# Moving the helper sums of an attention and PReLU kernel to VectorE, giving attention fixed units, and regrouping on ScalarE

## The chip, the cores and the metric

The kernel runs on one core of a Trainium2 chip. A core has five engines that run their own instruction streams in order and wait for each other through semaphores: TensorE (PE in the profile, its weight loads PEld), VectorE (DVE), ScalarE (ACT), GpSimd (POOL) and SyncE (SP). The metric is device time of one execution in microseconds. Before the change the median of 10 runs is 315.63 us (314.99 to 317.3).

## The reference

Attention without a softmax, with a norm on each head's output, then a two-layer PReLU network over the concatenated heads. All inputs are float32, the output is float32 of 4608 x 512.

```python
batch, n_heads, seq, head_dim = (8, 8, 576, 64)
kv  = einsum('bhsd,bhse->bhde', k, v)
o   = einsum('bhsd,bhde->bhse', q, kv)
o   = o / sqrt(mean(o*o, -1) + 1e-6) * g_norm
x   = o.transpose(0, 2, 1, 3).reshape(4608, 512)
h   = x @ w_in                                # 512 -> 2048
g   = maximum(h, 0) + alpha * minimum(h, 0)
out = g @ w_out                               # 2048 -> 512
```

## The kernel before

The 4608 tokens are cut into 9 blocks of 512 (w = 0 to 8); the tokens of a block can come from two of the eight batches. Everything on TensorE is fp16, accumulated in fp32.

**Attention of a block** goes by four head pairs j, each in four steps. `step_t` (L232) transposes q of the pair with 5 matmuls into `qt_ps`, and ACT copies it to `qt_sb`. `step_kv` (L250) makes k^T v with 5 matmuls into `kv_ps`, and DVE masks it into `kv_sb`. `step_ot` (L268) makes the outputs with 2 matmuls into `ot_ps`, and ACT squares them (`sq_sb`). `step_ssq` (L286) sums the squares with one matmul into `ssq_ps`, ACT makes the reciprocal root (`rstd`), and DVE writes the normed block part `xt`. `window_steps` (L308) lists these 16 steps in one order, in which the last `ssq` follows the last `ot` directly. From stage two on `qt_ps` and `kv_ps` share the one PSUM bank of the pool `ps_s`; `ssq_ps` has the bank of `ps_q` up to the loop of block 1, and from the loop of block 2 that of `ps_s` as well.

**First layer of a block**: 16 units. `m1_group` (L351) runs 4 matmuls of 512 columns into a bank `h_ps`; ACT makes `m_sb = relu(-h)` (L342) and DVE writes the activation `gt = beta * m_sb + h` in fp16 (L346). A bank can be filled again when DVE has read it. There are three banks until block 2, and two (`h0`, `h1`) from then on.

**Second layer of block 0**: four output tiles of 128 tokens, 16 matmuls each. Three (`ya`, `yb`, `yc`, AHEAD = 3) run in "stage two", between the first layers of blocks 0 and 1, with the attention steps of block 1 in between; the fourth (`y_ps`) runs in the loop of block 1.

**Second layer of blocks 1 to 8**: by Winograd's form of Strassen's product, with 7 products of 16 matmuls of 256 columns (`prod_mm`, L461) into three banks yX, yY, yZ. The products need sums of parts of the weights (`w_sum`, L404: 4 kinds in two halves) and of parts of the activations (`s_sum`, L428: 4 kinds for 4 parts, so 16 for a block). In the loop of block w each unit has one `m1_group` of block w, the sums that are due, 7 matmuls of the products of block w - 1, a read of a finished bank (`y_read`, L494), and attention steps of block w + 1, popped from their list as the units go by. After block 8 a tail runs its products alone.

**Where the sums run before**: on POOL all eight `w_sum` (L407 to L419; the third kind overwrites part of `w_out_sb`), all sums of the third kind (L437), and in block 1 those of the fourth kind (L440). The others run on DVE (L433, L435, L440).

**Loading**: `load_batch(b)` issues six DMAs from the POOL queue (three of 64 KB for the last 64 rows, three of 512 KB). k and q arrive head by head, and `regroup` (L142) copies them into the order that the matmuls need: of batches 0 and 1 on DVE, of batch 2 on POOL after stage two (`regroup_batch`, L155), of later batches on POOL in units 10 and 12 of the loop of block b - 2, one copy of 2048 elements a partition for k and one for q. POOL thus has, in one in-order stream, DMA issues, regroup copies and sums. Results are stored from the SP queue.

Of the kernel before, what the change touches and what calls it, by code (L numbers as in the profile page):

```python
# [17 lines left out]
def kernel(  # L18
# [11 lines left out]
    nc = tc.nc  # L30
# [111 lines left out]
    def regroup(b, nm, h0, h1, eng=None):  # L142
        dst = bufs[b % NBUF][nm][:, 0:TPP, h0:h1, :].rearrange("p t h d -> p h t d")
        src = stages[b, nm][:, h0:h1, :, :]
        if eng is nc.scalar:
            nc.scalar.copy(out=dst, in_=src)
        else:
            (eng or nc.vector).tensor_copy(out=dst, in_=src)
# [247 lines left out]
    def w_lo(i, c0, c1):  # L396
        return w_out_sb[i][:, :, c0:c1]
# [3 lines left out]

    def w_sum(n, i):
        sl = slice(i * GW, (i + 1) * GW)
        if n != 3 and n not in wsum:  # L404
            wsum[n] = w_p.tile([P, NK, HC], FP16, name=f"wsum{n}")
        if n == 1:
            nc.gpsimd.tensor_sub(  # L407
                out=wsum[1][:, sl, :], in0=w_lo(i, HC, D_MODEL), in1=w_lo(i, 0, HC)
            )
        elif n == 2:  # L410
            nc.gpsimd.tensor_sub(  # L411
                out=wsum[2][:, sl, :], in0=w_hi(i, HC, D_MODEL), in1=wsum[1][:, sl, :]
            )
# [12 lines left out]
    def s_sum(w, n, k):  # L426
        lo, hi = gts[w, k], gts[w, k + KQ]
        a11, a21 = lo[:, :, 0:HW], lo[:, :, HW:W]  # L428
        a12, a22 = hi[:, :, 0:HW], hi[:, :, HW:W]
        t = sum_p.tile([P, 2, HW], FP16, name=f"s{n}", tag=f"s{n}{k}", bufs=1 if n == 2 else 2)  # L430
        sums[w, n, k] = t
        if n == 1:
            nc.vector.tensor_add(out=t[:], in0=a21, in1=a22)  # L433
        elif n == 2:
            nc.vector.tensor_sub(out=t[:], in0=sums[w, 1, k][:], in1=a11)  # L435
# [25 lines left out]
    def prod_mm(w, n, i):  # L461
        a, c = divmod(i, NK)
        bank, fresh = y_bank(w, {1: "X", 2: "X", 6: "Y", 7: "Y", 4: "Y", 5: "Z", 3: "Z"}[n], a)
        cols = slice(a * P, (a + 1) * P)
        hi_cols = slice(HW + a * P, HW + (a + 1) * P)
        k, r = divmod(c, 2)
        if n == 1:
            lhs = gts[w, k][:, r, cols]
        elif n == 2:
            lhs = gts[w, k + KQ][:, r, cols]  # L470
        elif n == 4:
            lhs = gts[w, k + KQ][:, r, hi_cols]
        else:
            lhs = sums[w, {6: 2, 7: 3, 5: 1, 3: 4}[n], k][:, r, cols]
        q, rr = divmod(c, GW)
        if n == 1:
            rhs = w_out_sb[q][:, rr, 0:HC]
        elif n == 2:
            rhs = w_out_sb[q + WQ // 2][:, rr, 0:HC]
        elif n == 3:  # L480
            rhs = w_out_sb[q + WQ // 2][:, rr, HC:D_MODEL]
        elif n == 7:
            rhs = w_out_sb[q][:, rr, HC:D_MODEL]
        else:
            rhs = wsum[{4: 4, 5: 1, 6: 2}[n]][:, c, :]
        nc.tensor.matmul(  # L486
            out=bank, lhsT=lhs, rhs=rhs, start=fresh, stop=(c == NK - 1), skip_group_check=True,
        )
# [80 lines left out]
    for g in range(3, NF):  # L569
# [5 lines left out]


    AHEAD = 3
    ys = [
        ps_y.tile([P, W], FP32, name="ya", tag="y"),
        h_bank("yb"),  # L580
        h_bank("yc"),
    ]
    steps = window_steps(1)
    n = len(steps)
    for g in range(NF):
        for a in range(AHEAD):
            y_mm(ys[a], 0, a, g)
            if a != 1 and steps and n - len(steps) < n * (AHEAD * g + a + 1) // (AHEAD * (NF - 3)):
                steps.pop(0)()
    for a in range(AHEAD):  # L590
        y_out(ys[a], 0, a)
    regroup_batch(2)

    def unit_sums(w, u):
        k, r = divmod(u, 4)
        k -= 1
        if k >= 0 and r < 3:
            s_sum(w, (1, 2, 4)[r], k)
            if r == 0:
                s_sum(w, 3, k)  # L600

    for w in range(1, NW):
        steps = window_steps(w + 1) if w + 1 < NW else []
        n = len(steps)
        first_g = 4 if w == 1 else 0
        if w == 2:
            h_tags[0] = ("h0", "h1")
            ssq_pool[0] = (ps_s, "s")
            for i in range(2):
                w_sum(3, i)  # L610
        if 0 < w and w + 2 < B:
            load_batch(w + 2)
        if w == 1:
            for i in range(2):
                for m in (1, 2, 4):
                    w_sum(m, i)
        y = None
        for u in range(NF):
            m1_group(w, G_ORDER[u])
            unit_sums(w, u)  # L620
            if w > 1 and u < 3:
                unit_sums(w - 1, NF + u)
# [63 lines left out]
```

## Time and profile before

| | us |
|---|---|
| median of 10 runs | 315.63 |
| the profiled execution | 316.04 |
| its span (first to last instruction) | 314.2 |
| PE busy | 283.9 (90%) |
| DVE busy | 218.4 (70%) |
| ACT busy | 161.0 (51%) |
| POOL busy | 128.1 (41%) |

Two clocks must be kept apart: the time that is measured (316.04 us for the profiled execution) and the span inside it (314.2 us) in which positions are given; the 1.84 us around it belong to both kernels. Positions below are microseconds from the span's start. A matmul's time in the profile runs until its modelled end, and matmuls overlap, so what a group of matmuls costs is read from the distance between starts. The same holds, to a smaller degree, for instructions that follow each other on DVE and ACT. The granted TensorE clock was 0.987 over the span.

### The profile page before, as it was taken

How to read it: one execution, taken by the hardware profiler on the slowest of the kernel's cores; microseconds unless marked ns; L12 is line 12 of the kernel's file. 1: busy time of each engine (PE TensorE's matmuls, PEld its weight loads, DVE VectorE, ACT ScalarE, POOL GpSimd, SP SyncE). 2: the span in 40 equal slices, each digit the busy share in tenths (PEclk: the TensorE clock that was granted, in tenths of full speed). 3: DMA queues.
4: the chain of work that ended last, by engine and by line, in shares of the span. 5: the costliest groups of instructions: out<-in, count | busy, mean ns of one | idle time of the engine just before them, and what ended most of it. 6: DMA issues, size and time to landing. Idle time of an engine off the chain costs nothing.

```text
span 314.2 us, 5166 instructions
## 1 busy us (share of the span) xinstructions
PE 283.9 (90%) x1972; PEld 180.1 (57%) x1972; DVE 218.4 (70%) x373; ACT 161.0 (51%) x268; POOL 128.1 (41%) x118
## 2 busy tenths in 40 slices
PE   5778999696697999999999999999999999999992
PEld 1523454343374657665766576656665666666682
DVE  4358833778768886888688768876777778866831
ACT  3246556385454556555655555555654565434210
POOL 8434412999999551365136413311111112211100
PEclk9599999999999999999999999999999999999999
DMA  7999999790039299029902990111102110200233
GB/s 110 180 206 195 200 198 215 106 158 2 33 28 183 52 144 182 2 40 156 167 18 26 157 162 9 26 67 34 37 1 52 50 33 11 75 19 33 63 89 85
DMA packets 52552, 28.32 MB, mean 90 GB/s; under 512 B 15136, under 2 KB 52016, under 8 KB 52528
## 3 DMA queue, kind: packets, MB, share of 16 engines
q0 software_dynamic: 40320, 18.16, 45.9%
q1 hardware_dynamic: 11424, 9.19, 10.3%
q10 hardware_dynamic: 784, 0.66, 0.8%
q8 instruction: 15, 0.25, 0.3%
q14 instruction: 9, 0.07, 0.1%
HBM read 36.71 MB, written 9.44 MB: 147 GB/s over the span
## 4 chain that ended last, share of the span: by engine, by line
PE 63%; DMA 14%; POOL 11%; DVE 4%; issue 4%; ACT 2%; DVEq 0%; POOLq 0%
PE h_ps L335 28%; PE yY L486 11%; PE yZ L486 9%; PE yX L486 8%; DMA qst<-in_q_dram 5%; DMA kst<-in_k_dram 5%; DMA vst<-in_v_dram 3%; PE qt_ps L236 2%; PE kv_ps L254 2%; PE ssq_ps L293 2%; PE ot_ps L277 2%; POOL wsum L407 1%; POOL wsum L411 1%; POOL wsum L415 1%; ACT m_sb L342 1%
## 5 line engine op out<-in xcount | busy, mean ns | idle before, releaser
L335 PE MATMUL h_ps<-xt,w_in_sb 128*128 128x512 f16 x576 | 146.1, 379 | 2.2 <-DVE gt L346 1.2
L346 DVE SCALAR_TENSOR_TENSOR gt<-m_sb,beta_sb,h_ps 128x512 f16<-128x512 f32 x144 | 107.1, 745 | 57.5 <-ACT m_sb L342 55.9
L342 ACT ACTIVATE m_sb<-h_ps 128x512 f32<-128x512 f32 x144 | 85.9, 597 | 78.5 <-PE h_ps L335 71.0
L437 POOL TENSOR_TENSOR s<-gt 128x512 f16<-128x512 f16 x32 | 39.0, 1219 | 134.0 <-DVE gt L346 133.7
L335 PEld LDWEIGHTS <-w_in_sb 128*128 128x128 f16 x576 | 54.2, 98 | 54.0 <-issue 9.8
L486 PEld LDWEIGHTS <-s 128*128 128x128 f16 x512 | 50.1, 98 | 22.9 <-DVE u L501 1.9
L486 PEld LDWEIGHTS <-gt 128*128 128x128 f16 x384 | 37.6, 98 | 14.8
L303 DVE SCALAR_TENSOR_TENSOR xt<-ot_ps,g2col,rstd 128x512 f16<-128x512 f32 x36 | 26.9, 747 | 12.5 <-ACT rstd L295 12.4
L486 PE MATMUL yX<-w_out_sb,gt 128*128 128x256 f16 x256 | 35.1, 273 | 0.0
L295 ACT ACTIVATE rstd<-ssq_ps,eps_t 128x512 f32<-128x512 f32 x36 | 24.7, 687 | 17.0 <-PE ssq_ps L293 16.8
L283 ACT ACTIVATE sq_sb<-ot_ps 128x512 f16<-128x512 f32 x36 | 21.3, 598 | 16.1 <-PE ot_ps L277 16.1
L248 ACT COPY qt_sb<-qt_ps 128x576 f16<-128x576 f16 x28 | 17.9, 638 | 18.4 <-PE qt_ps L236 18.4
L236 PE MATMUL qt_ps<-ident,qsb 128*128 128x128 f16 x160 | 14.9, 231 | 7.5 <-DVE kv_sb L262 4.2
L486 PE MATMUL yY<-w_out_sb,s 128*128 128x256 f16 x128 | 18.7, 272 | 1.7 <-DVE u L501 1.6
L440 DVE TENSOR_TENSOR s<-gt,s 128x512 f16<-128x512 f16 x28 | 19.4, 692 | 0.0
L433 DVE TENSOR_TENSOR s<-gt 128x512 f16<-128x512 f16 x32 | 19.3, 602 | 0.0
L293 PE MATMUL ssq_ps<-sq_sb,mask 128*128 128x512 f16 x36 | 13.9, 386 | 5.9 <-ACT sq_sb L283 4.5
L236 PEld LDWEIGHTS <-qsb 128*128 128x128 f16 x160 | 12.0, 103 | 11.4 <-issue 4.8
L486 PE MATMUL yZ<-w_out_sb,s 128*128 128x256 f16 x128 | 17.5, 272 | 0.7 <-DVE y_sb L513 0.3
L486 PE MATMUL yY<-wsum,s 128*128 128x256 f16 x128 | 17.6, 273 | 0.0
L486 PE MATMUL yY<-wsum,gt 128*128 128x256 f16 x128 | 17.6, 273 | 0.0
L486 PE MATMUL yZ<-wsum,s 128*128 128x256 f16 x128 | 17.6, 273 | 0.0
(66 smaller groups left out, 263.5 us busy)
## 6 DMA issues: line engine op xcount, KB each, us to landing
out_dram<-y_sb SPq DMA_DIRECT2D x72, 64.0 KB, 2.2
kst<-in_k_dram POOLq DMA_DIRECT2D x7, 512.0 KB, 6.3
qst<-in_q_dram POOLq DMA_DIRECT2D x7, 512.0 KB, 12.5
vst<-in_v_dram POOLq DMA_DIRECT2D x7, 512.0 KB, 9.4
out_dram<-y_sb SPq DMA_DIRECT2D x23, 128.0 KB, 2.1
w_in_sb<-in_moe_w_in_dram POOLq DMA_DIRECT2D x4, 512.0 KB, 14.5
w_out_sb<-in_moe_w_out_dram POOLq DMA_DIRECT2D x4, 512.0 KB, 16.9
out_dram<-y_sb SPq DMA_DIRECT2D x4, 256.0 KB, 3.2
```

The costliest lines, as they stand in the source:

```text
L236: nc.tensor.matmul(out=qt_ps[:, t * P : (t + 1) * P], lhsT=qs(t), rhs=ident16[:], is_transpose=True, start=(t == 0), stop=(t == NT - 1),)
L283: nc.scalar.activation(out=sq[:], in_=ot_ps[:], func=AF.Square)
L293: nc.tensor.matmul(out=ssq_ps[:], lhsT=mask16[:], rhs=sq[:], start=True, stop=True)
L295: nc.scalar.activation(out=rstd[:], in_=ssq_ps[:], func=AF.Abs_reciprocal_sqrt, bias=eps_t[:], scale=inv_d,)
L303: nc.vector.scalar_tensor_tensor(out=xts[w, j][:], in0=ot_ps[:], scalar=g2col[:], in1=rstd[:], op0=ALU.mult, op1=ALU.mult,)
L335: nc.tensor.matmul(out=h_ps[:], lhsT=w_in_blk(c, g), rhs=xts[w, c][:], start=(c == 0), stop=(c == NC - 1),)
L342: nc.scalar.activation(out=m_sb[:], in_=h_ps[:], func=AF.Relu, scale=-1.0)
L346: nc.vector.scalar_tensor_tensor(out=gts[w, i][:, r, :], in0=m_sb[:], scalar=beta_sb[:, g : g + 1], in1=h_ps[:], op0=ALU.mult, op1=ALU.add,)
L433: nc.vector.tensor_add(out=t[:], in0=a21, in1=a22)
L437: nc.gpsimd.tensor_sub(out=t[:], in0=a11, in1=a21)
L440: eng.tensor_sub(out=t[:], in0=a12, in1=sums[w, 2, k][:])
L486: nc.tensor.matmul(out=bank, lhsT=lhs, rhs=rhs, start=fresh, stop=(c == NK - 1), skip_group_check=True,)
```

## The change

- `w_sum` and `s_sum`: all sums run on VectorE. The third kind of weight sum gets a tile of its own in place of overwriting `w_out_sb`, and the seventh product reads it there. Six of the eight weight sums now stand in stage two, the other two in units 9 and 15 of block 1. The buffers of the activation sums become two for kinds 1 and 2, one for 3 and 4.
- Activation sums follow a table (`S_AT`): 16 in the 14 units 0 to 13, at most two in a unit.
- Attention steps follow a table: `t` at unit 3j, `kv` at 3j + 1, `ot` at 3j + 3, `ssq` at 3j + 5; in the loop of block 1 another one (`ATT_1`).
- Stage two: of the third tile `yc` eight matmuls run there with the others, four more after them, and the last four in units 0 to 3 of block 1 beside the fourth tile (now `yd`). The attention list of block 1 is popped after any of the matmuls, and ends four matmuls before the end. From block 1 on there are two banks `h_ps`, and `ssq_ps` uses the bank of `ps_s`.
- `regroup` runs on ScalarE by head pair, in eight copies of 512 elements a partition for a batch: batch 2 in units 0, 1 and 3 to 6 of block 1, batch w + 2 in units 8 to 15 of block w. POOL is left with DMA issues.

```diff
-    def regroup_batch(b):
-        for nm in ("k", "q"):
-            regroup(b, nm, 0, H, nc.gpsimd)
+    def regroup_pair(b, nm, j):
+        regroup(b, nm, 2 * j, 2 * j + 2, nc.scalar)
...
-            nc.gpsimd.tensor_sub(
-                out=w_lo(i, HC, D_MODEL), in0=w_hi(i, HC, D_MODEL), in1=w_lo(i, HC, D_MODEL),
+            nc.vector.tensor_sub(
+                out=wsum[3][:, sl, :], in0=w_hi(i, HC, D_MODEL), in1=w_lo(i, HC, D_MODEL),
             )
...
-            nc.gpsimd.tensor_sub(out=t[:], in0=a11, in1=a21)
+            nc.vector.tensor_sub(out=t[:], in0=a11, in1=a21)
         else:
-            eng = nc.gpsimd if w == 1 else nc.vector
-            eng.tensor_sub(out=t[:], in0=a12, in1=sums[w, 2, k][:])
+            nc.vector.tensor_sub(out=t[:], in0=a12, in1=sums[w, 2, k][:])
...
     AHEAD = 3
+    SPLIT = 8
+    FILL = 4
...
+    T_AT = {5: (1, 0), 7: (1, 1), 9: (2, 0), 11: (4, 0), 13: (2, 1), 15: (4, 1)}
+    total = 2 * NF + SPLIT
+    done = 0
     for g in range(NF):
-        for a in range(AHEAD):
+        for a in range(AHEAD if g < SPLIT else AHEAD - 1):
             y_mm(ys[a], 0, a, g)
-            if a != 1 and steps and n - len(steps) < n * (AHEAD * g + a + 1) // (AHEAD * (NF - 3)):
+            done += 1
+            if steps and n - len(steps) < n * done // (total - 4):
                 steps.pop(0)()
-    for a in range(AHEAD):
-        y_out(ys[a], 0, a)
-    regroup_batch(2)
+        if g in T_AT:
+            w_sum(*T_AT[g])
+    while steps:
+        steps.pop(0)()
+    y_out(ys[1], 0, 1)
+    y_out(ys[0], 0, 0)
+    for g in range(SPLIT, SPLIT + FILL):
+        y_mm(ys[2], 0, 2, g)
+    h_tags[0] = ("h0", "h1")
+    h_turn[0] = 0
+    ssq_pool[0] = (ps_s, "s")
+
+    S_AT = {
+        0: ((-1, 1, 3),), 1: ((-1, 2, 3),), 2: ((-1, 3, 0),), 3: ((-1, 3, 1), (-1, 3, 2)),
+        4: ((-1, 3, 3),), 6: ((0, 1, 0), (0, 2, 0)), 7: ((-1, 4, 0),), 8: ((-1, 4, 1),),
...
+    for j in range(NPAIR):
+        for what, at in (("t", 0), ("kv", 1), ("ot", 3), ("ssq", 5)):
+            ATT_AT.setdefault(3 * j + at, []).append((what, j))
...
+        for what, at in (("kv", 1 + j), ("t", 4 + 2 * j), ("ot", 6 + 2 * j), ("ssq", 8 + 2 * j)):
+            ATT_1.setdefault(at, []).append((what, j))
...
+    REG_2 = {0: (("k", 0), ("k", 1)), 1: (("k", 2), ("k", 3))}
+    REG_2.update({3 + j: (("q", j),) for j in range(NPAIR)})
+    REG_AT = {8 + 2 * j + i: ((nm, j),) for j in range(NPAIR) for i, nm in ((0, "q"), (1, "k"))}
```

Three places show how instructions move; names with a number are one buffer of a tile. In the changed kernel's file the same code stands one to four lines further up, so L342 of before is L341 of after, and so on.

The first is TensorE at the last attention steps of a block in the loop of block 3. Before:

```order
L277 MATMUL ot_ps<-qt_sb,kv_sb 128x256
L277 LDWEIGHTS kv_sb
L277 MATMUL ot_ps<-qt_sb,kv_sb 128x256
L293 LDWEIGHTS mask_112
L293 MATMUL ssq_ps<-sq_sb,mask_112 128x512
L335 LDWEIGHTS w_in_sb_164
L335 MATMUL h_ps<-xt,w_in_sb_164 128x512
```

After, at the same `ot`:

```order
L276 MATMUL ot_ps<-qt_sb,kv_sb 128x256
L276 LDWEIGHTS kv_sb
L276 MATMUL ot_ps<-qt_sb,kv_sb 128x256
L334 LDWEIGHTS w_in_sb_160
L334 MATMUL h_ps<-xt,w_in_sb_160 128x512
```

The `ssq` that stood behind the `ot` now comes two units later, with eight first-layer matmuls and fourteen of the products between them.

The second is ScalarE in the later half of the loop of block 1, where `qsb_135` and `ksb_131` are batch 3 in its regrouped order. Before:

```order
L342 ACTIVATE m_sb<-h_ps 128x512 x2
L295 ACTIVATE rstd<-ssq_ps,eps_t 128x512
L248 COPY qt_sb<-qt_ps 128x576
L342 ACTIVATE m_sb<-h_ps 128x512
L283 ACTIVATE sq_sb<-ot_ps 128x512
L342 ACTIVATE m_sb<-h_ps 128x512
```

After, units 7 to 10:

```order
L341 ACTIVATE m_sb<-h_ps 128x512 x2
L294 ACTIVATE rstd<-ssq_ps,eps_t 128x512
L282 ACTIVATE sq_sb<-ot_ps 128x512
L247 COPY qt_sb<-qt_ps 128x576
L146 COPY qsb_135<-qst 128x2x4x64
L341 ACTIVATE m_sb<-h_ps 128x512
L146 COPY ksb_131<-kst 128x2x4x64
L341 ACTIVATE m_sb<-h_ps 128x512
```

Between the relu of unit 8 and that of unit 9 there are now four other ACT instructions, one of them a copy that waits for the q of batch 3 to land.

The third is VectorE at the start of the loop of block 3, whose sums belong to block 2. Before:

```order
L433 TENSOR_TENSOR s_1387<-gt 128x512
L513 TENSOR_TENSOR y_sb<-yZ,u_1100 128x512
L346 SCALAR_TENSOR_TENSOR gt<-m_sb,beta_sb,h_ps 128x512
L435 TENSOR_TENSOR s_1421<-s_1387,gt 128x512
L262 TENSOR_TENSOR kv_sb<-kv_ps,mask_108 128x128
L346 SCALAR_TENSOR_TENSOR gt<-m_sb,beta_sb,h_ps 128x512
L440 TENSOR_TENSOR s_1447<-gt,s_1421 128x512
```

After:

```order
L432 TENSOR_TENSOR s_1394<-gt 128x512
L509 TENSOR_TENSOR y_sb<-yZ,u_1099 128x512
L345 SCALAR_TENSOR_TENSOR gt<-m_sb,beta_sb,h_ps 128x512
L434 TENSOR_TENSOR s_1426<-s_1394,gt 128x512
L261 TENSOR_TENSOR kv_sb<-kv_ps,mask_108 128x128
L345 SCALAR_TENSOR_TENSOR gt<-m_sb,beta_sb,h_ps 128x512
L436 TENSOR_TENSOR s_1452<-gt 128x512
L345 SCALAR_TENSOR_TENSOR gt<-m_sb,beta_sb,h_ps 128x512
L436 TENSOR_TENSOR s_1472<-gt 128x512
L436 TENSOR_TENSOR s_1474<-gt 128x512
```

The sums of the third kind (L436), which stood in POOL's stream, now stand between the `gt` of units 2 to 4; the fourth kind follows in units 7 to 10.

More of the change, by code (lines that the diff above doesn't have):

```diff
@@ new lines, with attention @@
+    ATT_1 = {}
+    for j in range(NPAIR):
+        for what, at in (("kv", 1 + j), ("t", 4 + 2 * j), ("ot", 6 + 2 * j), ("ssq", 8 + 2 * j)):
+            ATT_1.setdefault(at, []).append((what, j))
+    ATT = {"t": step_t, "kv": step_kv, "ot": step_ot, "ssq": step_ssq}
+    def attention(w, u):
+        if w < NW:
+            for what, j in (ATT_1 if w == 2 else ATT_AT).get(u, ()):
+                if w < B or what in ("ot", "ssq"):
+                    ATT[what](w, j)
+    REG_2 = {0: (("k", 0), ("k", 1)), 1: (("k", 2), ("k", 3))}
@@ L644 @@
     for u in range(NF):
-        if u < 3:
-            unit_sums(w, NF + u)
+        unit_sums(NW, u)
         if u == 0:
```

70 lines of the change are left out of this document (30 added, 40 removed), and 2 rows, old and new, of the table S_AT.

## The prediction

> **What bounds the kernel now.** First I read busy times by stage, the stages cut where the first layer of a block begins. Columns: stage, its length, then busy us (instructions) of PE, PEld, DVE, ACT, POOL, granted clock, DMA engines' busy share, GB/s.
>
> ```profile
> 36.50:52.36 15.86, 14.98 (x101) 7.74 (x100) 6.14 (x11) 8.31 (x14) 3.99 (x4) 1.00 1.43 198
> 52.36:80.69 28.33, 22.10 (x134) 11.05 (x132) 21.34 (x29) 17.60 (x31) 25.02 (x18) 1.00 0.67 98
> 80.69:116.65 35.96, 30.87 (x228) 20.29 (x228) 27.68 (x39) 18.72 (x32) 30.29 (x26) 1.00 0.72 90
> 116.65:147.75 31.10, 30.40 (x231) 20.62 (x228) 24.27 (x42) 18.02 (x31) 13.41 (x12) 1.00 0.63 92
> 210.08:241.25 31.17, 30.40 (x231) 20.40 (x229) 22.28 (x42) 18.02 (x31) 4.71 (x4) 1.00 0.12 36
> ```
>
> These are stage two and the loops of blocks 1, 2, 3 and 6. Blocks 2, 3 and 6 do the same work on PE, yet block 2 takes 35.96 us and the others 31.1. Blocks 1 and 2 are also the ones where POOL is busy nearly throughout (25.02 of 28.33, 30.29 of 35.96). In blocks 3 to 6 PE is busy for all but 0.7 us. So there are two questions: what blocks 1 and 2 wait for, and how much is left in the others.
>
> PE's rows in time give the cost of each piece as the distance between starts. Columns: start, us, engine, line, operation, tile, count.
>
> ```profile
> 53.44 1.03 PE L335 MATMUL h_ps<-xt,w_in_sb 128*128 128x512 f16 x4
> 54.52 1.03 PE L335 MATMUL h_ps<-xt,w_in_sb 128*128 128x512 f16 x4
> ...
> 116.65 1.03 PE L335 MATMUL h_ps<-xt,w_in_sb 128*128 128x512 f16 x4
> 118.28 0.44 PE L236 MATMUL qt_ps<-ident,qsb 128*128 128x128 f16 x5
> 118.56 1.03 PE L335 MATMUL h_ps<-xt,w_in_sb 128*128 128x512 f16 x4
> 120.19 0.39 PE L254 MATMUL kv_ps<-vst,ksb 128*128 128x128 f16 x4
> 120.47 1.03 PE L335 MATMUL h_ps<-xt,w_in_sb 128*128 128x512 f16 x4
> ...
> 143.22 0.38 PE L277 MATMUL ot_ps<-qt_sb,kv_sb 128*128 128x256 f16 x2
> 144.28 0.38 PE L293 MATMUL ssq_ps<-sq_sb,mask 128*128 128x512 f16 x1 [0.69 <-ACT sq_sb L283]
> 144.50 1.02 PE L335 MATMUL h_ps<-xt,w_in_sb 128*128 128x512 f16 x4
> ```
>
> A unit of first layer and products is 118.28 - 116.65 = 1.63 us, a `t` 0.28, a `kv` 0.28, an `ssq` 0.22; `ot` has the same 512 columns and gets 0.22 too. A block is then 16 x 1.63 + 4 x (0.28 + 0.28 + 0.22 + 0.22) = 30.1 us. Block 3 takes 31.10, and its one large wait is visible: the last `ssq` starts 1.06 us behind its `ot` and not 0.22, since ACT must first square. That is 0.84 us. A unit of block 1 is 54.52 - 53.44 = 1.08.
>
> Now the waits of blocks 1 and 2, on PE, DVE and POOL together:
>
> ```profile
> 58.74 0.70 POOL L137 DMA_DIRECT2D vsb<-in_v_dram  x1
> 60.96 0.92 POOL L131 DMA_DIRECT2D qst<-in_q_dram  x1
> 59.04 2.17 DVE L433 TENSOR_TENSOR s<-gt 128x512 f16<-128x512 f16 x1
> 62.12 0.28 DVE L262 TENSOR_TENSOR kv_sb<-kv_ps,mask 128x128 f16<-128x128 f32 x1
> 62.45 0.44 PE L236 MATMUL qt_ps<-ident,qsb 128*128 128x128 f16 x5 [2.89 <-DVE kv_sb L262]
> ...
> 84.95 0.45 PE L236 MATMUL qt_ps<-ident,qsb 128*128 128x128 f16 x5 [2.48 <-POOL qsb L148]
> 95.44 2.35 DVE L435 TENSOR_TENSOR s<-s,gt 128x512 f16<-128x512 f16 x1
> 98.45 0.28 PE L486 MATMUL yY<-w_out_sb,s 128*128 128x256 f16 x1 [1.62 <-DVE u L501]
> ```
>
> The first two rows are the first and the last of four DMA issues that stand back to back on POOL. A sum beside them takes 2.17 us on DVE, `kv_sb` comes behind it, and the transpose that needs `kv_ps`'s bank stands on PE for 2.89 us. Block 2 waits 2.48 us for a regroup copy that was late in POOL's stream, and 1.62 us behind a sum of 2.35 us. A sum with POOL at rest, or out of its way, is far shorter:
>
> ```profile
> 141.26 0.75 DVE L346 SCALAR_TENSOR_TENSOR gt<-m_sb,beta_sb,h_ps 128x512 f16<-128x512 f32 x1 [0.59 <-ACT m_sb L342]
> 141.93 0.42 DVE L433 TENSOR_TENSOR s<-gt 128x512 f16<-128x512 f16 x1
> 142.26 0.68 DVE L513 TENSOR_TENSOR y_sb<-yZ,u 128x512 f32<-128x512 f32 x1
> 142.86 0.74 DVE L303 SCALAR_TENSOR_TENSOR xt<-ot_ps,g2col,rstd 128x512 f16<-128x512 f32 x1
> ```
>
> By starts: `gt` 0.67, a sum 0.33, a read of a bank 0.60.
>
> **Part one: the sums on VectorE.** A block on DVE becomes 16 `gt` x 0.67 + 4 `xt` x 0.67 + 16 sums x 0.33 + 5 reads x 0.60 + 4 `kv_sb` x 0.28 = 22.8 us of about 30, and no unit has more than two sums: the fullest, with `gt`, a read and `xt`, is 1.94 us against 1.84 to 1.91 of PE. So DVE is no bound as long as a sum costs 0.33. How far a late `gt` may slip, these rows tell (the unit that starts at 120.47):
>
> ```profile
> 121.53 0.60 ACT L342 ACTIVATE m_sb<-h_ps 128x512 f32<-128x512 f32 x1 [1.31 <-DVE kv_sb L262]
> 122.16 0.75 DVE L346 SCALAR_TENSOR_TENSOR gt<-m_sb,beta_sb,h_ps 128x512 f16<-128x512 f32 x1 [0.62 <-ACT m_sb L342]
> ```
>
> The bank is read 122.91 - 120.47 = 2.44 us after the unit began and wanted two units later, after 3.3 to 4 us: a slack of some 1.2 us. The unknown is whether POOL's DMA issues still stretch sums. Six issues of 0.7 to 0.92 us are 4.8 us of a 30 us loop, so 16 x 4.8 / 30 = 2.6 sums in each of the five loops that load meet one. The sum at 141.93 ran in 0.42 us beside an issue, the one at 59.04 took 2.17. One in three stretched to 2.17 would cost 2.17 - 0.42 - 1.2 = 0.55 us in about one place a loop, nothing where the slack is larger. The bounds are 0 and 5 x 2.6 x 0.55 = 7.2 us; I take **1.0 us**, nearer the short rows, since more of the rows beside issues that I looked at are short.
>
> The Trainium skill speaks to this (SBUF — State Buffer, Who interferes with whom): a DVE instruction with two SBUF inputs contends with a GpSimd instruction that reads SBUF, and descriptor generation is inferred to need only the write side. By that rule the 1.0 us would be 0 and the time 1.0 us lower. The row at 59.04 speaks against it, since nothing but DMA issues ran beside that sum.
>
> The six weight sums in stage two have twice the elements and are put at 0.7 us each; DVE is busy for 6.14 of 15.86 us there, so they cost nothing unless one stands before the last `xt`.
>
> **Part two: attention at fixed units.** With `ssq` two units behind `ot` the 0.84 us goes. Nothing is late in its place: the last `ssq` stands in unit 14, so its `xt` has unit 15 (1.63 us) and three matmuls of the next block to be ready. Blocks 3 to 6: 4 x 0.84 = **3.4 us**. Block 2, with its regroup moved and sums short, becomes such a block: 31.10 - 0.84 = 30.3, so 35.96 - 30.3 = **5.7 us**. Blocks 7 and 8 and the tail have no such wait, so I leave them.
>
> **Part three: stage two and block 1.** Four matmuls of `yc` leave stage two: 4 x 0.22 = 0.9, so block 1 starts at 51.5. Its PE work is 16 x 1.08 + 4 x 0.22 + 4.0 = 22.2 us. Here new waits come in, from ACT. Its rows:
>
> ```profile
> 99.05 0.64 ACT L248 COPY qt_sb<-qt_ps 128x576 f16<-128x576 f16 x1 [2.24 <-PE qt_ps L236]
> 99.58 0.60 ACT L283 ACTIVATE sq_sb<-ot_ps 128x512 f16<-128x512 f32 x1
> 100.13 0.60 ACT L342 ACTIVATE m_sb<-h_ps 128x512 f32<-128x512 f32 x1
> 100.62 0.58 ACT L507 COPY y_sb<-yX 128x512 f32<-128x512 f32 x1
> ...
> L295 ACT ACTIVATE rstd<-ssq_ps,eps_t 128x512 f32<-128x512 f32 x36 | 24.7, 687 | 17.0 <-PE ssq_ps L293 16.8
> ```
>
> By starts: `qt_sb` 0.53, `sq_sb` 0.55, relu 0.49; `rstd`, busy 0.69, is taken as 0.62. A regroup copy on ACT is not in the trace; the copies beside it bound it by 0.49 and 0.69, and I take 0.53, that of `qt_sb` with 576 elements. Block 1 has sixteen of them, since batches 2 and 3 are both copied there. In its units 8 to 15 ACT has 8 x 0.49 + 4 x 0.62 + 3 x 0.55 + 2 x 0.53 + 8 x 0.53 + 0.5 = 13.9 us, and PE 8 x 1.08 + 7 x 0.22 + 2 x 0.28 = 10.7. With two banks PE can't run ahead: **3.1 us** go there. In unit 4 `t` and `kv` stand side by side and share the bank of `ps_s`: `kv` waits until ACT has done a relu, a regroup copy and `qt_sb`, some **1.4 us**. Block 1 is then 22.2 + 4.5 = 26.7 us and ends at 78.2 in place of 80.69: **2.5 us** saved. If a copy costs 0.49 or 0.69 the later half moves by -0.3 or +1.3.
>
> From block 2 on ACT has 18.02 + 8 x 0.53 = 22.3 us of 30, at most 2.1 us in a unit with 2.13 us of PE, so the copies are hidden there by PE. POOL is left with DMA issues, and loads can only be issued earlier.
>
> **The sum**, against the profiled execution's own 316.04 us (0.4 above the median): 316.04 - 3.4 - 5.7 - 2.5 + 1.0 = **305.4 us**.
>
> **The rivals.**
>
> *Sums stretched throughout by DMA issues*: all 13 sums that meet one cost 0.55: 7.2 in place of 1.0, so 311.6 us. For it: 2.17 at 59.04. Against: 0.42 at 141.93. Chance 0.13.
>
> *ACT waits for batch 3*. ACT wants its q in unit 8 of block 1, behind a bit more than half of the loop at about 67.8. Before, the DMA engines finished that batch at 70:
>
> ```profile
> 66.00:70.00 4.00, 4.00 (x27) 2.07 (x26) 3.95 (x7) 3.06 (x6) 3.92 (x3) 1.00 1.44 177
> 70.00:72.00 2.00, 0.66 (x8) 0.47 (x7) 2.00 (x4) 0.96 (x3) 1.92 (x2) 1.00 0.04 6
> ```
>
> Its `v` and `q` were then issued at 58.74 and 60.96 (rows above), behind two POOL copies that are gone, so it should land some us earlier. If it lands at 70 all the same, ACT and the units behind it wait 2.3 us: 307.7 us. Chance 0.12.
>
> *Block 1 runs at PE's pace*: ACT's copies slip into gaps and the 4.5 us don't come, nor the 1.0: 299.9 us. Chance 0.14.
>
> *DVE becomes the bound, slower than before.* Sixteen sums a block stand on the engine that must also free the two banks. DVE has 30.3 - 22.8 = 7.5 us to spare in a block, so from 0.33 + 7.5 / 16 = 0.80 us a sum on it sets the pace, and from about 1.7 us a block beyond that, 0.91 us a sum in the mean over seven blocks, the whole 11.6 us are lost. At the 2.17 us of the row above a block would be 52 us. It takes DMA issues that stretch most sums and not one in three: 4.8 us of issues a loop are too short for that. Chance 0.04.
>
> *Nothing gained*: the waits of blocks 1 and 2 were covers for others of the same length, 316 us. PE's own 30.1 us a block speaks against it. Chance 0.02.
>
> **How the numbers follow.** The forecast, 302 to 309, has 0.55. Faster by over 0.2% is every case but the last two: 0.94; the same 0.02; slower 0.04 (0.2% is about what a measurement of this kernel can tell from no change). The range 300 to 311 leaves out half of the first and of the third rival and the last two: 0.07 + 0.07 + 0.06 = 0.2.
>
> **What the profile would show.** Right: loops of blocks 2 to 6 of 30.2 to 30.6 us with no wait of PE for `sq_sb`; sums of 0.42 us but for one or two a loop; block 1 near 26.7 us with ACT nearly full in its later half, and PE waiting for `qt_sb` in unit 4. Wrong: sums of over 1 us in numbers, PE waiting for `gt` in blocks 3 to 8, or ACT idle in block 1 behind a DMA.

## The result and the profile after

The changed kernel takes 303.33 us (median of 8 runs, 302.59 to 304.32); the kernel before, run beside it, 315.55 us (28 runs). The ratio is 0.9609, 95% interval [0.9594, 0.9624]. The profiled execution of the changed kernel took 304.32 us with a span of 302.5, the longest of its eight. Further below, the profiled run of the kernel with only the sums moved (328.08 us) was 1.9% above that kernel's fastest, so its time and ratio are those of its three other runs and only its block lengths are from the profiled one.

First the busy times by stage, as in the prediction. The stages are block 1, a part of it (the second row), and blocks 2, 3 and 6.

```profile
52.33:78.71 26.38, 23.08 (x137) 11.47 (x136) 17.82 (x32) 23.38 (x45) 6.25 (x8) 1.00 1.29 173
66.70:79.00 12.30, 10.20 (x55) 4.72 (x54) 9.53 (x17) 12.22 (x25) 0.00 (x0) 1.00 1.00 118
78.71:109.14 30.43, 30.18 (x229) 20.55 (x229) 24.27 (x46) 21.87 (x40) 4.69 (x6) 1.00 0.56 74
109.14:139.55 30.41, 30.16 (x230) 20.62 (x228) 24.00 (x46) 21.43 (x39) 4.72 (x6) 1.00 0.65 95
200.38:230.57 30.19, 30.18 (x231) 20.34 (x229) 24.02 (x46) 18.62 (x32) 0.00 (x0) 1.00 0.12 36
```

Block 2 now looks like block 3, POOL's column has only DMA issues in it, and in the later half of block 1 ACT is busy for 12.22 of 12.30 us. The two profiled executions differ by 316.04 - 304.32 = 11.72 us, their spans by 11.7, and the starts of the blocks say where:

| stretch | before | after | difference | forecast |
|---|---|---|---|---|
| up to the start of block 1, and block 1 (to its end) | 80.69 | 78.71 | -1.98 | -2.5 |
| block 2 | 35.96 | 30.43 | -5.53 | -5.7 |
| blocks 3 to 6 | 124.60 | 121.43 | -3.17 | -3.4 |
| blocks 7, 8 and tail | 72.95 | 71.93 | -1.02 | 0 |
| sums stretched by DMA issues | | | 0 | +1.0 |

What PE still waits for in blocks 1 and 2 (rows in time; the bracket holds the idle time before the row and what ended it):

```profile
61.16 0.38 PE L253 MATMUL kv_ps<-vst,ksb 128*128 128x128 f16 x4 [1.20 <-ACT qt_sb L247]
67.45 0.44 PE L235 MATMUL qt_ps<-ident,qsb 128*128 128x128 f16 x5 [0.61 <-ACT rstd L294]
71.22 0.44 PE L235 MATMUL qt_ps<-ident,qsb 128*128 128x128 f16 x5 [0.73 <-ACT rstd L294]
77.26 1.02 PE L334 MATMUL h_ps<-xt,w_in_sb 128*128 128x512 f16 x4 [0.54 <-DVE gt L345]
78.71 1.04 PE L334 MATMUL h_ps<-xt,w_in_sb 128*128 128x512 f16 x4 [0.22 <-DVE gt L345]
...
105.45 0.38 PE L482 MATMUL yZ<-w_out_sb,s 128*128 128x256 f16 x2 [0.25 <-DVE y_sb L509]
```

The 2.89, 2.48 and 1.62 us of before are gone, and so is the wait for `sq_sb` in the loops. New are five waits of block 1, 3.3 us together, three of them for ACT and two for DVE, and a small one of 0.25 us for `yZ` that returns once in each of blocks 2 to 5. The sums, grouped by line (columns: busy us, mean ns of one), and one of them beside the DMA issue under which it ran:

```profile
L434 DVE TENSOR_TENSOR s<-s,gt 128x512 f16<-128x512 f16 x32 | 13.5, 421 | 0.5
L432 DVE TENSOR_TENSOR s<-gt 128x512 f16<-128x512 f16 x32 | 13.4, 418 | 0.0
L438 DVE TENSOR_TENSOR s<-gt,s 128x512 f16<-128x512 f16 x32 | 13.2, 418 | 0.0
L436 DVE TENSOR_TENSOR s<-gt 128x512 f16<-128x512 f16 x32 | 12.6, 418 | 0.0
```

```profile
132.31 0.91 POOL L131 DMA_DIRECT2D qst<-in_q_dram  x1
132.72 0.42 DVE L432 TENSOR_TENSOR s<-gt 128x512 f16<-128x512 f16 x1
```

None of the 128 sums is stretched. Eleven of them ran beside a DMA issue of POOL, and each took 0.42 us.

### The profile page after: what moved, and what is told of

Read it like the earlier page. It is cut to its first block, busy times and chain, and to the rows that moved or that the text cites. A ratio compares the mean times of both kernels' runs of the same rounds, so it can differ in the third digit from the quotient of the medians.

```text
span 302.5 us, 5167 instructions
## 1 busy us (share of the span) xinstructions
PE 282.3 (93%) x1972; PEld 180.4 (60%) x1972; DVE 220.7 (73%) x417; ACT 181.4 (60%) x316; POOL 44.2 (15%) x62
## 2 busy tenths in 40 slices
DMA packets 52553, 28.33 MB, mean 94 GB/s; under 512 B 15136, under 2 KB 52016, under 8 KB 52528
## 4 chain that ended last, share of the span: by engine, by line
PE 80%; ACT 7%; DVE 5%; issue 3%; DMA 2%; SPq 1%; DVEq 0%
PE h_ps L334 35%; PE yY L482 12%; PE yZ L482 10%; PE yX L482 9%; PE qt_ps L235 3%; PE kv_ps L253 3%; ACT m_sb L341 3%; PE ssq_ps L292 2%; DMA alpha_row<-in_moe_alpha_dram 2%; PE ot_ps L276 2%; DVE gt L345 2%; ACT rstd L294 1%; ACT ksb L146 1%; PE yc L359 1%; DVE y_sb L509 1%
## 5 line engine op out<-in xcount | busy, mean ns | idle before, releaser
L341 ACT ACTIVATE m_sb<-h_ps 128x512 f32<-128x512 f32 x144 | 86.2, 600 | 65.4 <-PE h_ps L334 49.7
L482 PE MATMUL yY<-wsum,s 128*128 128x256 f16 x256 | 36.3, 273 | 0.0
L131 POOL DMA_DIRECT2D vst<-in_v_dram x9 | 7.7, 858 | 63.3 <-PE kv_ps L253 59.9
L253 PEld LDWEIGHTS <-ksb 128*128 128x128 f16 x160 | 11.9, 101 | 6.1 <-issue 2.9
L146 ACT COPY qsb<-qst 128x512 f16<-128x512 f16 x24 | 14.8, 617 | 0.0
L146 ACT COPY ksb<-kst 128x512 f16<-128x512 f16 x24 | 14.8, 624 | 0.0
```

Of the source, the lines that this page charges most:

```text
L253: nc.tensor.matmul(out=kv_ps[:], lhsT=ks(t), rhs=vs(t), start=(t == 0), stop=(t == NT - 1),)
L341: nc.scalar.activation(out=m_sb[:], in_=h_ps[:], func=AF.Relu, scale=-1.0)
L482: nc.tensor.matmul(out=bank, lhsT=lhs, rhs=rhs, start=fresh, stop=(c == NK - 1), skip_group_check=True,)
```

## The experiments

Ratios are to the kernel before, run beside each kernel, with the 95% interval. Block lengths are distances between the first `h_ps` matmuls of the blocks, in the profiled executions:

| kernel | median us | ratio | block 1 | 2 | 3 | 4 |
|---|---|---|---|---|---|---|
| before | 315.55 | 1 | 28.33 | 35.96 | 31.10 | 31.16 |
| after | 303.33 | 0.9609 [0.9594, 0.9624] | 26.38 | 30.43 | 30.41 | 30.42 |
| before, only copies moved | 312.07 | 0.9883 [0.9845, 0.9921] | 29.62 | 31.57 | 31.10 | 31.17 |
| before, only sums moved | 323.31 | 1.0254 [1.018, 1.0327] | 32.99 | 34.26 | 34.06 | 36.97 |
| after, POOL sums back | 308.59 | 0.9771 [0.9727, 0.9815] | 30.19 | 31.01 | 31.0 | 31.41 |
| after, copies back on POOL | 311.97 | 0.9882 [0.9839, 0.9924] | 25.58 | 32.26 | 33.92 | 34.36 |
| after, old attention list | 306.7 | 0.9712 [0.9678, 0.9745] | 26.38 | 31.04 | 31.03 | 31.03 |
| after, block 1's edits together | 299.99 | 0.95 [0.9477, 0.9524] | 24.65 | 30.10 | 30.08 | 30.09 |

### The two moves apart, on the kernel before

Only the regroup copies go to ACT:

```diff
-    regroup_batch(2)
...
-            if w + 2 < B and u in (10, 12):
-                regroup(w + 2, "k" if u == 10 else "q", 0, H, nc.gpsimd)
...
+            if w + 2 < B:
+                for nm, j in REG_AT.get(u, ()):
+                    regroup(w + 2, nm, 2 * j, 2 * j + 2, nc.scalar)
```

(and batch 2's copies in units 0, 1 and 3 to 6 of block 1).

> The kernel before with one part of the change alone: regroup copies of batches 2 and on go to ACT by head pair, at the units of the changed kernel; POOL keeps its sums, and stage two and the attention list stay as before. Theory: POOL's copies were what made block 2 late and what stretched DVE's sums there, so block 2 falls from 36 us to 31 to 32.5, block 1 stays near 28 because POOL's weight sums and the third-kind sums still read SBUF beside DVE, and blocks 3 to 6 keep their 31.1: 310 to 312.5 us. Rival: POOL's sums alone keep DVE's stretched in block 2 as well, block 2 stays over 34 us and the time at 314 or more.

The theory's time and block 2 came, with 312.07 us and 31.57; block 1 got longer, 29.62 and not 28. So of block 2's 5.53 us the copies alone bring 35.96 - 31.57 = 4.39. Block 1's rows on POOL, DVE and PE (three views, one under the other) show what was left there:

```profile
59.53 2.30 POOL L407 TENSOR_TENSOR wsum<-w_out_sb 128x1024 f16<-128x1024 f16 x1
```

```profile
60.43 1.68 DVE L435 TENSOR_TENSOR s<-s,gt 128x512 f16<-128x512 f16 x1
62.03 0.28 DVE L262 TENSOR_TENSOR kv_sb<-kv_ps,mask 128x128 f16<-128x128 f32 x1
```

```profile
62.36 0.69 PE L236 MATMUL qt_ps<-ident,qsb 128*128 128x128 f16 x5 [2.87 <-DVE kv_sb L262]
```

This is the wait of 2.89 us that the prediction read at 62.45 in the kernel before, and this time a weight sum runs on POOL all along. POOL's operation ends at 59.53 + 2.30 = 61.83, DVE's sum at 60.43 + 1.68 = 62.11, 0.28 us later; `kv_sb` and the transpose stand behind it.

The wait has a second price here. In the first of the two stretches below PE does little; in the second the granted clock (the number behind POOL's busy time) is 0.50:

```profile
58.88:62.29 3.41, 0.60 (x6) 0.32 (x5) 3.41 (x4) 1.13 (x3) 3.33 (x3) 1.00 1.56 195
62.29:65.71 3.42, 3.35 (x13) 1.66 (x13) 0.30 (x2) 1.55 (x3) 3.34 (x2) 0.50 1.16 151
```

At half the clock 3.35 us of PE are some 1.7 us of work, so about 1.7 us of block 1's 29.62 are this, and the 28 of the theory is left. In the kernel before the wait of 2.89 us is followed by no such stretch.

Only the sums go to DVE:

```diff
-            nc.gpsimd.tensor_sub(out=t[:], in0=a11, in1=a21)
+            nc.vector.tensor_sub(out=t[:], in0=a11, in1=a21)
...
-            eng = nc.gpsimd if w == 1 else nc.vector
+            eng = nc.vector
```

(and the same for the four forms of `w_sum`).

> The kernel before, with all sums on DVE and nothing else changed: regroup copies stay on POOL, six weight sums stand at the start of block 1. Theory (POOL's sums both stretched DVE's and delayed the regroup copies in blocks 1 and 2): most of these two blocks' 8 us come back, and the loops of blocks 3 to 6 stay at 31.1 us: 307 to 310 us. Rival (the sums alone only move the load, and spacing and regroup give the gain): 313 us or more.

The theory's band was missed by 13 us, and the time is past that of the kernel before. PE's waits between 40 and 235 us (columns: total, times, longest):

```profile
PE yZ L486 <- DVE y_sb L513: 8.6, 4, 3.0
PE h_ps L335 <- DVE gt L346: 4.0, 4, 2.7
```

The sums on VectorE alone are a loss of 8.0 us (a ratio of 1.0254, interval 1.018 to 1.0327). The blocks of the profiled run overstate it: 6.8 us of block 1 and 6.8 us of block 4 ran at a clock of 0.50, behind waits of 2.6 to 3.1 us. With the copies still on POOL, DVE holds more work that can be held up, and what stands behind a held sum is the bank read or the `gt` that PE needs next.

### The two moves taken back, in the changed kernel

The sums that ran on POOL before go back, apart from the fourth kind of block 1:

```diff
-            nc.vector.tensor_sub(out=t[:], in0=a11, in1=a21)
+            nc.gpsimd.tensor_sub(out=t[:], in0=a11, in1=a21)
```

(and the same for `w_sum`).

> The changed kernel with the sums of the third kind and the eight weight sums back on POOL, at their new places. Theory (a POOL instruction that reads SBUF and a sum on DVE exclude each other): sums on DVE that meet a POOL sum take 1 us and more, mostly in block 1 and in units 2 to 4 of each loop; with only some of them met and a slack of 1.2 us PE loses little from block 3 on: 303 to 306 us, the loss in stage two and blocks 1 and 2. Rival (the sums cost nothing on either engine, and the gain of blocks 1 and 2 is the removal of regroup copies from POOL's stream): 303.3, and no stretched sums.

The direction is the theory's, the size was more: 308.59 us, and most of it in block 1 (26.38 to 30.19), where a wait of 2.31 us also brought 3.41 us at a clock of 0.50. The regroup copies go back whole:

```diff
-                for nm, j in REG_AT.get(u, ()):
-                    regroup_pair(w + 2, nm, j)
+            if w + 2 < B and u in (10, 12):
+                regroup(w + 2, "k" if u == 10 else "q", 0, H, nc.gpsimd)
```

(and batch 2 on POOL ahead of block 1).

> The changed kernel with the regroup copies back on POOL (two copies of 2048 elements a batch; batch 2 ahead of block 1). Theory (a POOL instruction that reads SBUF stretches the sums on DVE, and ACT's sixteen copies are what holds block 1 back in its later half): sums beside a copy take 1.3 to 1.6 us again, some two in each of the loops 1 to 5; ACT is relieved, so block 1 loses about 1 us less, and PE's 0.25 us wait for the read of yZ in blocks 2 to 5 goes; in all 301 to 303.5 us against 303.3. Rival (the copies on ACT are hidden, and what the change gained is that POOL no longer stretches sums): 304.5 us or more, with PE waiting for gt behind stretched sums.

311.97 us: the loss that the rival named, and larger. Block 1 alone gained 0.8 us, with no copies on ACT; blocks 2, 3 and 4 lost 1.8, 3.5 and 3.9 us. First a pair of rows from the kernel with the sums back, on POOL and on DVE:

```profile
109.59 1.21 POOL L436 TENSOR_TENSOR s<-gt 128x512 f16<-128x512 f16 x1 [0.39 <-DVE gt L345]
```

```profile
109.81 1.26 DVE L434 TENSOR_TENSOR s<-s,gt 128x512 f16<-128x512 f16 x1
```

Then the rows of POOL, DVE and PE from the loop of block 3 with the copies back:

```profile
132.49 0.89 POOL L131 DMA_DIRECT2D qst<-in_q_dram  x1
133.36 1.91 POOL L148 COPY ksb<-kst 128x2048 f16<-128x2048 f16 x1
```

```profile
132.89 2.67 DVE L432 TENSOR_TENSOR s<-gt 128x512 f16<-128x512 f16 x1
```

```profile
137.87 0.38 PE L482 MATMUL yZ<-w_out_sb,s 128*128 128x256 f16 x2 [2.07 <-DVE y_sb L509]
```

```profile
134.90:138.31 3.41, 1.34 (x11) 0.85 (x10) 3.41 (x6) 0.71 (x2) 0.37 (x1) 1.00 1.55 187
138.31:141.73 3.42, 3.42 (x13) 1.77 (x12) 2.22 (x5) 0.61 (x2) 1.24 (x1) 0.50 0.67 137
```

The wait of 2.07 us, where the changed kernel has 0.25, is 1.8 of block 3's 3.5 us; the other 1.7 are the half clock behind it. Block 4 is the same with a wait of 2.52 us; in block 2 a wait of 2.08 us is followed by the full clock, and 1.8 us are all that it loses.

Ends minus ends: 111.07 - 110.80 = 0.27, and 135.56 - 135.27 = 0.29. That is the same 0.28 us as above. In the kernel before, the two kernels with one part moved alone, and the two with the sums or the copies back on POOL, 45 sums on DVE take over 0.6 us. Forty-two of them end 0.27 to 0.30 us after a POOL copy or sum has ended, whether that took 1.2 or 2.3 us; the other three stand beside DMA issues alone. A sum is thus not slowed by POOL but held until POOL's operation is over. It goes the other way round too: with only the copies moved, 27 sums on POOL begin 0.16 to 0.26 us behind a sum on DVE. DVE's takes its 0.42 us, and POOL's ends 1.01 to 1.02 us after it, whatever the distance of the two starts. The Trainium skill (SBUF — State Buffer, Who interferes with whom) has the port that both engines read through as an exclusive lock, which goes to whoever issues first. These ends and the pair at 109.59 agree with it; at 132.89 the sum's record begins ahead of the copy's, and there the order of the records does not fit.

### What on POOL holds a sum

Both kernels are the changed one with four extra POOL instructions in each unit, on a tile that nothing else uses:

```diff
+    pool_b = const_p.tile([P, W // 2], FP16, name="pool_b")
...
+            for _ in range(4):
+                nc.gpsimd.tensor_copy(out=pool_b[:], in_=warm16[:, 0 : W // 2])
```

> The changed kernel with four extra POOL copies of 256 fp16 elements a partition (SBUF to SBUF, into a tile that nobody reads) in each unit of the loops of blocks 1 to 8; nothing else waits for them. Theory (a POOL instruction that reads SBUF and a sum with two SBUF inputs exclude each other): sums on DVE take well over 0.42 us wherever POOL copies run, most of them over 0.6, gt (one SBUF input) stays at 0.75. Rival (the stretched sums of before had another cause, as DMA issues): sums stay at 0.42 us.

The other has, in place of the copy, an operation that only writes and reads nothing:

```diff
+            for _ in range(4):
+                nc.gpsimd.memset(pool_b[:], 0.0)
```

> The same with four POOL memsets in place of the copies: POOL writes SBUF and reads nothing. Theory (only reads of SBUF by POOL hold the sums up, which is also why DMA issues don't): sums stay at 0.42 us and the time at 303.3 us. Rival (any work of POOL does): sums as long as with the copies.

The groups, with the copies:

```profile
L644 POOL COPY pool_b<-warm 128x256 f16<-128x256 f16 x512 | 220.9, 431 | 31.4
...
L438 DVE TENSOR_TENSOR s<-gt,s 128x512 f16<-128x512 f16 x32 | 15.5, 490 | 0.0
L434 DVE TENSOR_TENSOR s<-s,gt 128x512 f16<-128x512 f16 x32 | 15.5, 484 | 0.5
```

and with the writes alone:

```profile
L644 POOL MEMSET pool_b<- 128x256 f16 x512 | 160.0, 313 | 29.0
...
L434 DVE TENSOR_TENSOR s<-s,gt 128x512 f16<-128x512 f16 x32 | 13.5, 422 | 0.5
```

POOL busy for 160 us with writes leaves a sum at 422 ns and the time at 303.74 us. Copies raise it to a mean of 484, by no more than a part of one short copy of 431. That the sums are held is the theory's; that most take over 0.6 us is not: 18 of 128 do, the longest 0.66, and `gt` stays at 0.75. What a hold costs is set by the length of the POOL instruction: the regroup copies were of 1.9 us. The kernel with the copies is slow all the same, 327.34 us (1.0376 [1.0346, 1.0406]), for another reason. PE's and ACT's waits:

```profile
PE kv_ps L253 <- ACT qt_sb L247: 16.9, 5, 6.4
```

```profile
ACT qsb L146 <- DMA qst<-in_q_dram: 19.0, 4, 7.3
```

The loads are issued from POOL's queue, behind all those copies, and come late.

### The attention list

From the loop of block 2 on, the old list is popped again as before:

```diff
+        steps = window_steps(w + 1) if w > 1 and w + 1 < NW else []
+        n = len(steps)
...
-            attention(w + 1, u)
+            if w == 1:
+                attention(w + 1, u)
+            else:
+                want = n * (u + 1) // (NF - 2)
+                while steps and n - len(steps) < want:
+                    steps.pop(0)()
```

> The changed kernel with the attention steps from the loop of block 2 on popped from the old list as before; block 1 keeps the new table. Theory (each loop of blocks 2 to 6 lost 0.84 us to the ssq behind its ot): 5 x 0.7 to 0.84 us more, 306.8 to 307.5 us, with PE's wait for sq_sb of 0.69 us back once a loop. Rival (the spacing matters through the load on DVE and ACT, which are short now): 303.3 to 305.

306.7 us, 3.4 more than the changed kernel and just under the theory's band, and the wait is back, once a loop:

```profile
PE ssq_ps L292 <- ACT sq_sb L282: 3.7, 6, 0.7
```

Blocks 2 to 5 are 0.61 to 0.62 us longer each, since the 0.25 us for `yZ` goes in exchange, and block 6, which has no such wait, 0.85.

### Block 1

First, without the split of the third tile (all 16 matmuls of `yc` in stage two):

```diff
-    SPLIT = 8
-    FILL = 4
+    SPLIT = 16
+    FILL = 0
...
+    y_out(ys[2], 0, 2)
```

> The changed kernel with all sixteen matmuls of yc in stage two (no split). Theory (the split only moves 0.86 us of matmuls; ACT sets the end of block 1, but the four matmuls ahead of block 1 cover the wait for the last xt): block 1 begins as much later as it gets shorter, and PE waits for xt at its start: 303.3 to 304.3. Rival (the split gains the moved matmuls): 304.2 to 305.

304.53 us (0.9645 [0.9607, 0.9684]), which is the rival's band: by the medians the split brings 1.2 us, and by the profiles 0.87 from the start of stage two to the end of block 1. Without it block 1 does not get shorter but takes 26.70 us, with a new wait of 0.47 us for a regroup copy of k. Three edits then take one cover each from the waits of block 1. The `ssq` gets the idle bank of `yZ`:

```diff
-    ssq_pool[0] = (ps_s, "s")
...
+        if w == 2:
+            ssq_pool[0] = (ps_s, "s")
```

> The changed kernel with ssq_ps in block 1 in the bank that is idle there (that of yZ). Theory A (the shared bank delays PE in units 8 and 10, 0.61 + 0.73 us, but ACT is full in these units): PE's waits for rstd go, waits for gt grow in their place, and the time falls by 0.5 us or less, to 302.8 to 303.3. Rival B (PE's waits for the bank are the loss itself): 1.3 us less, 302.0.

The last `kv` goes to unit 3:

```diff
-        for what, at in (("kv", 1 + j), ("t", 4 + 2 * j), ("ot", 6 + 2 * j), ("ssq", 8 + 2 * j)):
+        for what, at in (("kv", j + (j < 3)), ("t", 4 + 2 * j), ("ot", 6 + 2 * j), ("ssq", 8 + 2 * j)):
```

> The changed kernel with the last kv of block 1 in unit 3 behind the third, and not behind the first t in unit 4. Theory (PE's 1.20 us wait for qt_sb in unit 4 is lost time, since ACT stands idle for 1.39 us right after it): 0.8 to 1.2 us less, 302.1 to 302.5. Rival (ACT's load of the whole block sets its end): PE gets ahead and waits for gt in units 12 to 15 instead, 303.0 to 303.3.

And batch 3's copies, in block 1 alone, go to DVE, where one takes 0.28 to 0.29 us:

```diff
-                    regroup_pair(w + 2, nm, j)
+                    regroup(w + 2, nm, 2 * j, 2 * j + 2, nc.vector if w == 1 else nc.scalar)
```

> The changed kernel with the eight copies of batch 3 in block 1 on DVE in place of ACT. Theory (ACT is the bound in units 8 to 15): the waits of PE for gt at the end of block 1 (0.54 + 0.22 us and some tenths) go and ACT gets idle time there; those for rstd in units 8 and 10 stay: 302.0 to 302.6. Rival (DVE copies fall behind POOL's DMA issues, or the copies delay gt): 303.3 or more, with PE waiting for gt in block 1 as long as now or longer.

They take 302.85, 303.3 and 302.98 us; block 1 is 26.10, 26.17 and 26.25 us, where the changed kernel has 26.38. None of the times is clear of the changed kernel's own runs (302.59 to 304.32). Each moved a wait more than it removed one. PE's waits, of the first kernel and then of the second:

```profile
PE h_ps L334 <- DVE gt L345: 1.6, 4, 0.7
```

```profile
PE kv_ps L253 <- ACT y_sb L386: 1.0, 1, 1.0
```

With the bank of its own, the waits for `rstd` (1.3 us) are gone and those for `gt` rise from 0.8 to 1.6; with `kv` in unit 3 it waits for another ACT instruction in place of `qt_sb`. That is theory A of the first; the second has its rival's time, but PE's waits for `gt` at the end of the block stay at 0.8 us. With the copies off ACT, ACT is busy for only 9.65 of the block's last 12.28 us (12.20 in the changed kernel), but the shared bank still makes the transposes wait for `rstd`, and the waits for `gt` stay at 0.8 us as well; the time lies between theory and rival. So ACT being full is not all of it.

The last kernel makes the three edits together, with the last `kv` in unit 5, and gives DVE's queue room by two more:

```diff
-        9: ((-1, 4, 2),), 10: ((-1, 4, 3),), 11: ((0, 1, 1),), 12: ((0, 2, 1),),
+        9: ((-1, 4, 2),), 10: ((-1, 4, 3),), 11: ((0, 1, 1),), 15: ((0, 2, 1),),
...
-            if w == 1 and u in (9, 15):
-                w_sum(3, 0 if u == 9 else 1)
+            if w == 1 and u in (2, 5):
+                w_sum(3, 0 if u == 2 else 1)
```

> The changed kernel with four edits together, all in the loop of block 1 but the first: batch 3's regroup copies in block 1 on DVE (from block 2 on they stay on ACT), the ssq of block 1 in the idle bank yZ, its four kv at units 1, 2, 3 and 5 in place of 1 to 4, the third kind of weight sum at units 2 and 5 in place of 9 and 15, and one sum of the second kind moved from unit 12 to 15 in every loop. Theory: each single edit only moved block 1's wait to the next of three covers (ACT's copies, the shared bank, DVE's queue). Taken away together, block 1 falls from 26.2 us to 23 to 24.5, the rest stays, and the time is 300.5 to 301.8 us. Rival: what is left is a chain of h_ps, relu and gt with two banks that none of the edits shortens: block 1 stays at 25.5 or more and the time at 302.4 or more.

299.99 us, 3.3 below the changed kernel, and the best here. The stages (block 1, its second half, blocks 2 and 3):

```profile
51.11:75.76 24.65, 23.23 (x137) 11.42 (x136) 19.04 (x38) 20.39 (x39) 6.26 (x8) 1.00 1.46 194
63.48:75.76 12.28, 11.76 (x63) 5.50 (x62) 10.45 (x23) 10.45 (x20) 1.32 (x2) 1.00 1.43 170
75.76:105.86 30.10, 30.10 (x229) 20.55 (x229) 24.02 (x47) 21.16 (x39) 4.69 (x6) 1.00 0.55 73
105.86:135.94 30.08, 30.08 (x230) 20.62 (x228) 24.01 (x46) 21.45 (x39) 4.70 (x6) 1.00 0.66 96
```

The time is a little below the theory's band, block 1 a little above its 24.5. In the second half ACT has 10.45 us and DVE too, where the changed kernel had 12.22 and 9.53. Blocks 2 and 3 have no wait left: 30.1 us is the sum of matmul times that the prediction added up for a block. Block 1 is 1.73 us shorter than in the changed kernel; which of the edits carries how much of that is not told apart by this run. From block 2 on only the sum in unit 15 differs, and blocks 2 to 5 are 0.33 us shorter each, blocks 6 and 7 0.17.

The run also tells something on the 0.25 us for `yZ`. In the changed kernel, ACT and DVE ahead of that wait:

```profile
102.57 0.61 ACT L146 COPY ksb<-kst 128x512 f16<-128x512 f16 x1
103.08 0.60 ACT L341 ACTIVATE m_sb<-h_ps 128x512 f32<-128x512 f32 x1
```

```profile
103.71 0.75 DVE L345 SCALAR_TENSOR_TENSOR gt<-m_sb,beta_sb,h_ps 128x512 f16<-128x512 f32 x1 [0.25 <-ACT m_sb L341]
104.38 0.42 DVE L434 TENSOR_TENSOR s<-s,gt 128x512 f16<-128x512 f16 x1
104.72 0.68 DVE L509 TENSOR_TENSOR y_sb<-yZ,u 128x512 f32<-128x512 f32 x1
```

The regroup copy stands ahead of the relu, so `gt` is late, and then a sum stands ahead of the bank's read. In block 6, with the same sum and no copies, there is no wait; in the last kernel, with the same copies and the sum in unit 15, there is none either. It takes both.

## Why the prediction came out as it did

The forecast was 305.4 us, the profiled execution gave 304.32 and the median 303.33: the mechanisms held, and two sizes were off by a microsecond each, both on the same side.

**What bounds it**: right. Blocks 1 and 2 were late by waits behind POOL's work, and block by block PE's own time is what is left; the last kernel shows it bare with 30.08 us.

**Block 2, -5.7**: measured -5.53. The copies alone brought 4.39 of it; the rest goes with the sums and with the attention list, whose wait is 0.69 us a loop.

**Blocks 3 to 6, -3.4**: measured -3.17, of which the old list, put back, takes 2.7 in these four blocks. Two things lie under this. Block 6, without copies, gained 31.17 - 30.19 = 0.98 us, more than the 0.84 of the wait; the rest is that of blocks 7 and 8 below. Blocks 3 to 5, with them, gained 0.69 to 0.76: "the copies are hidden there by PE" is not quite so, since with a sum ahead of the bank's read they cost some 0.25 us a loop.

**Stage two and block 1, -2.5**: measured -1.98. Block 1 itself was 26.38 us for 26.7 forecast, with the wait in unit 4 at 1.20 us for 1.4 and ACT full in the later half. What fell short was its start: 52.33 us in place of 51.5 in this profiled execution. Stage two itself became shorter by 0.62 of the 0.9, 15.24 us after 15.86, but it began at 37.09 and not at 36.50. Up to there the code did not change, and the other kernels here begin it between 35.34 and 36.74, so that part differs from run to run; it also fits that this execution is the longest of eight. ACT as the sole cause was too narrow: with the copies of batch 3 off ACT, PE's waits in block 1 are 3.2 us after 3.3. The bank that `t`, `kv` and `ssq` share is one other cover that the runs show; that DVE's queue is a third was argued, not tested alone. The rival that block 1 would run at PE's pace came neither in the changed kernel nor, fully, in the last one: 24.65 us against 22.2 of PE.

**Sums stretched by DMA issues, +1.0**: this step failed. It took the sum of 2.17 us at 59.04, which stands beside DMA issues, as a sample of what issues do. The runs show something else: sums are held by POOL instructions that read SBUF, until 0.28 us after their end, and in the changed kernel POOL has none. The page of the Trainium skill that the prediction set aside had it right for this kernel: its rule gave 0 and a time 1.0 us lower. What held the two sums of before, at 59.04 and 93.28, isn't shown; they end 0.21 and 0.33 us after the end of an issue of `qsb`. A third such sum, of 0.88 us at 167.10 in the kernel with the sums back on POOL, ends 0.84 us after one.

**Blocks 7, 8 and the tail, left at 0**: measured -1.02. Block 7 gives 0.13, block 8 0.35, and 0.54 lie between the start of the last product and the end of the span (7.62 us before, 7.08 after), where only the last reads and stores run. What blocks 7 and 8 gained, the prediction had not looked for: the first matmul of a product that goes into `yY` or `yZ` can start when DVE has read the bank, and in block 8 a sum stood ahead of that read. Block 8 before, on DVE and on PE, and after, on PE:

```profile
279.82 0.42 DVE L435 TENSOR_TENSOR s<-s,gt 128x512 f16<-128x512 f16 x1
280.15 0.68 DVE L501 TENSOR_TENSOR u<-yY,p 128x512 f32<-128x512 f32 x1
```

```profile
279.95 0.82 PE L486 MATMUL yX<-w_out_sb,gt 128*128 128x256 f16 x6
280.89 0.27 PE L486 MATMUL yY<-w_out_sb,s 128*128 128x256 f16 x1
```

```profile
269.14 0.82 PE L482 MATMUL yX<-w_out_sb,gt 128*128 128x256 f16 x6
269.79 0.27 PE L482 MATMUL yY<-wsum,s 128*128 128x256 f16 x1
```

The distance falls from 0.94 to 0.65 us; the first matmul of the last product into `yZ` comes 0.07 us sooner as well, and in blocks 6 and 7 both come 0.07 us sooner. For the 0.54 at the end no cause is known.

The other two rivals with chances of over a tenth did not come either: no sum was stretched, and ACT copied q of batch 3 without a wait for its landing. The rival in which DVE becomes the bound was the right danger in the wrong kernel: the same 16 sums a block on DVE cost 8.0 us net when POOL keeps its copies, as the kernel with only the sums moved shows.

## What to carry to other kernels

When two engines hold each other up at a port, moving half of the work from one to the other can lose: sums alone cost 8.0 us and copies alone brought 3.7, and the gain came when nothing that reads SBUF was left on POOL. Where a long row is to be used as a price, look for the instruction on the other engine that ends with it: ends that agree to 0.03 us over forty rows say more than an average. And where single fixes only move a wait, list all that cover it (here an engine, a bank and a queue) and take them away together.

## What the runs showed of the hardware

- A long VectorE sum of two SBUF operands ends 0.27 to 0.30 us after a POOL copy or sum has ended (42 of 45 sums of over 0.6 us, POOL operations of 1.2 to 2.3 us); 512 POOL writes of 313 ns each stretched none.
- The hold can begin ahead of the POOL copy's record: the sum at 132.89 would have ended at 133.31, and the copy is recorded from 133.36. Six sums, this one among them, began under the DMA issue just ahead of a copy, and were held to that copy's end. In the changed kernel, where no copy follows the issues, the same place took 0.42 us. Why is not settled.
- A regroup copy of 512 fp16 elements a partition took 0.62 us on ACT (0.51 from start to start) and 0.28 to 0.29 on DVE.
- Between start-up and tail the granted clock changes in steps of 3.41 us. Nine times in five kernels it fell to 0.50, each time behind such a stretch in which PE was busy for 1.40 us or less (0.60 of 3.41 with only the copies moved, 1.34 with the copies back). With 1.42 us (144.36 to 147.77 with only the sums moved), and with the 1.50 us of the kernel before around its wait of 2.89, it stayed at 1.00. A wait of 2 to 3 us can thus cost up to 1.7 us more, by where it falls on these steps.
